# Sums of an MLP's second layer: kept in SBUF and added by VectorE, or kept in DRAM and added by accumulating DMAs

## The chip, the cores and the metric

The kernel runs on one core of a Trainium2 chip, in one launch. Its time is the device time of an execution in microseconds (us). The number compared is a median over runs.

## The reference

Three layers follow one another, on 2 x 768 = 1536 tokens of 512 features, all in float32:

```python
x = attention(q, k, v)                  # window of 16 keys each side, and block summaries
h = x @ w_in                            # 512 -> 2048, "first layer"
g = np.maximum(h, 0.0) + np.log1p(np.exp(-np.abs(h)))
x2 = g @ w_out                          # 2048 -> 512, "second layer"
a = x2 @ w1                             # 512 -> 1024
b = x2 @ w2
out = (a * b @ w3) @ w_out2             # 1024 -> 1024 -> 512
```

The change touches how `x2` is summed.

## The kernel before

Matrix products run with float32 values split into a high and a low part, three matmuls in place of one (`mm3`, line 239). w3 and the last matrix are multiplied with each other once, "w34", so that the last layer is one product. The tokens are worked on in 3 chunks c of 512.

The second layer sums over 16 blocks of 128 features of g. PSUM (2 banks for the first layer, 4 for the second, 2 others) has no room for sums of all three chunks at once, so the blocks go in 4 groups of four. A stage s = 0 to 11 is one group (s // 3) of one chunk (s % 3). Within it, steps X{n}, n = 4s to 4s+3, add up in four banks, one for each output block o of 128 features. At the end of a stage the banks must be emptied before the next one can begin. X{4s+3} is the last step into the banks, X{4s+4} the first of the next stage.

Before, the step Xo{s}_{o} empties a bank into one of 12 rows r = 4c + o. These lie in four SBUF tiles `acc` of three rows each, which are held until the end of the second layer. In the first group, it is a copy (`X_first`: VectorE for even o, line 545, ScalarE for odd o, line 543). In the later groups VectorE adds the bank to its row (`X_out`, line 549). After that a row is split into high (`x2_hi`, line 554, ScalarE) and low parts (`x2_lo`, line 557, GpSimd). For chunks 1 and 2 the last layers use a scheme of seven products P1 to P7 in place of eight, for which VectorE forms sums of rows in place (`T_sum`, line 646), and their low parts (line 672).

The seven products are done for i = 0 to 7 (`prod`, line 710); P1_1 is product 1 of i = 1. Each has a PSUM bank, of four in turn. VectorE combines them (`plus`, line 726: U2, U3, U4, C11, C12, C22, C21), and whichever operation reads a bank last frees it. It also does what the next i needs: sums of the weight tiles (Sf, line 680, and Ss, line 687, with low parts Sl, line 694), the gating product Mb (line 730), the low part Pl of the gated values (line 739) and half of the output copies Oo (line 744).

All steps are sorted once, on the host, by a planner (`Order`) with a cost per step, a latency per engine and the number of buffers of each kind. It emits the steps in its order of start times, and every engine executes its own part of that in order. The steps of TensorE have given places. Temporary tiles of 128 x 512 come from one pool `tmp` of 4 buffers: the softplus values `tm` between the two layers, `pa`, `t1`, `u` and `osb` later. A step that takes a buffer waits until the last user of the one that had it before is done.

Of the kernel before, what the change touches and what calls it, by code (L numbers as in the profile page):

```python
# [8 lines left out]
F32 = mybir.dt.float32  # L9
# [5 lines left out]
ALU = mybir.AluOpType  # L15
# [8 lines left out]
class Order:  # L24
# [21 lines left out]
    def add(self, name, eng, cost, place, fn, needs=(), take=(), give=(), port=False, table=None, lead=0.0):  # L46
        assert name not in self.steps, name
        self.steps[name] = (eng, cost, place, fn, list(dict.fromkeys(d for d in needs if d)), list(take))
        self.extra[name] = (port or eng == "POOL", table, lead)
        for t, b in take:  # L50
            assert b not in self.owner, b
            self.owner[b] = t
        for b in give:
            self.users.setdefault(b, {})[name] = 1
# [150 lines left out]
def fused_kernel(ctx, tc, q, k, kwin, v, vb, w_in, w_out, w1, w2, w3, wo2, mask, sel, ident, out):  # L205
    nc = tc.nc
    P = 128
    B, NT, _, NP, _, _ = q.shape
# [5 lines left out]
    CH = 512  # L214
# [6 lines left out]
    tmp_p = ctx.enter_context(tc.tile_pool(name="tmp", bufs=4))  # L221
# [3 lines left out]
    acc_p = ctx.enter_context(tc.tile_pool(name="acc", bufs=4))  # L225
# [3 lines left out]
    dr = ctx.enter_context(tc.tile_pool(name="dr", bufs=1, space=bass.MemoryType.DRAM))  # L229

    w34_d = dr.tile([8, P, D], F32, name="w34_d")
    vs_d = [dr.tile([NBK, D], F32, name=f"vs_d{b}") for b in range(B)]

    def f(ap):
# [66 lines left out]
    xt = {}  # L301
# [187 lines left out]
    xps = {}  # L489
    acc = {}  # L490
    x2 = {}

    def step(n):

        return n // 12, n % 12 // 4, 4 * (n // 12) + n % 4
# [37 lines left out]


    def acc_row(r):
        if r // 3 not in acc:
            acc[r // 3] = acc_p.tile([P, 3, CH], F32, tag="acc", name="acc")
        return acc[r // 3][:, r % 3]

    def X_first(s, o):  # L540
        a, p = acc_row(4 * s + o), xps[s, o]
        if o % 2:
            nc.scalar.copy(a, p)
        else:
            nc.vector.tensor_copy(a, p)

    def X_out(s, o):
        a = acc_row(4 * (s % 3) + o)
        nc.vector.tensor_tensor(a, a, xps[s, o], ALU.add)

    def x2_hi(c, o):
        if c not in x2:
            x2[c] = xt_p.tile([P, 2, 4, CH], F32R, tag="xt", name="x2t")
        nc.scalar.copy(x2[c][:, 0, o], acc_row(4 * c + o))

    def x2_lo(c, o, eng):
        eng.tensor_tensor(x2[c][:, 1, o], acc_row(4 * c + o), f(x2[c][:, 0, o]), ALU.subtract)
# [87 lines left out]
    def T_sum(t, k):  # L645
        sub = lambda d, a, b: nc.vector.tensor_tensor(d, a, b, ALU.subtract)
        if t == 1:
            tf[1, k] = tmp_p.tile([P, CH], F32, tag="tmp", name="t1")
            sub(tf[1, k], acc_row(8 + k), acc_row(4 + k))
        elif t == 3:  # L650
            sub(acc_row(8 + k), acc_row(10 + k), acc_row(8 + k))
        elif t == 2:
            sub(acc_row(10 + k), acc_row(10 + k), tf[1, k])
        else:
            sub(acc_row(6 + k), acc_row(6 + k), acc_row(10 + k))

    def T_hi(t, k):
        if (t, 0) not in tt:
            if t == 1:
                tt[1, 0] = acc_p.tile([P, 2, CH], F32R, tag="acc", name="t1h")  # L660
                tt[1, 1] = st_p.tile([P, 2, CH], F32R, tag="st", name="t1l")
            elif t == 3:
                tt[3, 0], tt[3, 1] = rows(2, 0, 0), rows(2, 1, 0)
            else:
                y = xt_p.tile([P, 2, 4, CH], F32R, tag="xt", name="t24")
                for a in range(2):
                    tt[2, a], tt[4, a] = y[:, a, 0:2], y[:, a, 2:4]
        nc.scalar.copy(tt[t, 0][:, k], tf[1, k] if t == 1 else acc_row({3: 8, 2: 10, 4: 6}[t] + k))

    def T_lo(t, k):  # L670
        src = tf[1, k] if t == 1 else acc_row({3: 8, 2: 10, 4: 6}[t] + k)
        nc.vector.tensor_tensor(tt[t, 1][:, k], src, f(tt[t, 0][:, k]), ALU.subtract)
# [75 lines left out]
    def O_store(c, m):  # L748
# [5 lines left out]
    o = Order({"h": 2, "x": 4, "a": 2, "xt": 3, "wi": 6, "wo": 6, "g": 4, "tmp": 4, "st": 4, "cv": 3, "acc": 4,  # L754
               "kw": 3, "q": 3, "s": 3, "b": 8, "c": 2})
    add = o.add
# [150 lines left out]
    for j in jobs:  # L907
        kind, i, p = j
# [60 lines left out]
    for n in range(N1):  # L969
        g, c, i = step(n)  # L970
# [13 lines left out]
    for s_ in range(12):  # L984
        g, c = divmod(s_, 3)
        for o_ in range(4):
            r = 4 * c + o_
            if g == 0:
                add(f"Xo{s_}_{o_}", "ACT" if o_ % 2 else "DVE", .6, None, lambda s_=s_, o_=o_: X_first(s_, o_),
                    (f"X{4*s_+3}_{o_//2}", f"Xo{(r-r%3)//4}_{(r-r%3)%4}" if r % 3 else None),  # L990
                    () if r % 3 else [("acc", f"acc{r//3}")], (f"x{s_}_{o_}",))
            else:
                add(f"Xo{s_}_{o_}", "DVE", .68, None, lambda s_=s_, o_=o_: X_out(s_, o_),
                    (f"X{4*s_+3}_{o_//2}", f"Xo{s_-3}_{o_}"), (), (f"x{s_}_{o_}",))
            if g == 3 and (c < 2 or o_ > 1):
                add(f"x2h{c}_{o_}", "ACT", .62, None, lambda c=c, o_=o_: x2_hi(c, o_),
                    (f"Xo{s_}_{o_}", o_ % 2 and f"x2h{c}_{o_-1}", c < 2 and o_ and f"x2h{c}_0"), () if o_ != 2 * (c == 2) else [("xt", f"y{c}")])
                add(f"x2l{c}_{o_}", "POOL", 1.3, None, lambda c=c, o_=o_: x2_lo(c, o_, nc.gpsimd),
                    (f"x2h{c}_{o_}",), (), (f"acc{r//3}",), lead=2)


    for r in range(16):
        p, jp = divmod(r, 4)
# [3 lines left out]
    for i in range(8):  # L1007
        p = i // 2
# [3 lines left out]
        p = ("acc", "st", "wi", "wi", "wi", "wi", "c", "c")[i]  # L1012
# [15 lines left out]

    A = lambda *rs: sorted({f"acc{r//3}" for r in rs})
    for k_ in range(2):  # L1030
        add(f"T1s{k_}", "DVE", .68, None, lambda k_=k_: T_sum(1, k_), (f"Xo11_{k_}", f"Xo10_{k_}"),
            [("tmp", f"tx{k_}")], A(8 + k_, 4 + k_), port=True)
        add(f"T3s{k_}", "DVE", .68, None, lambda k_=k_: T_sum(3, k_), (f"T1s{k_}", f"Xo11_{2+k_}"), (), A(8, 9, 10, 11), port=True)
        add(f"T2s{k_}", "DVE", .68, None, lambda k_=k_: T_sum(2, k_), (f"T3s{k_}", f"x2l2_{2+k_}"), (), A(10, 11), port=True)
        add(f"T4s{k_}", "DVE", .68, None, lambda k_=k_: T_sum(4, k_), (f"T2s{k_}", f"x2l1_{2+k_}"), (), A(6, 7, 10, 11), port=True)
        for t, src, tk in ((1, [f"tx{k_}"], [("acc", "t1h"), ("st", "t1l")]), (3, A(8 + k_), []), (2, A(10 + k_), [("xt", "y3")]), (4, A(6 + k_), [])):
            first_ = k_ == 0 and t in (1, 2)
            add(f"T{t}h{k_}", "ACT", .62, None, lambda t=t, k_=k_: T_hi(t, k_),
                (f"T{t}s{k_}", "x2h2_2", k_ and f"T{t}h0", t == 1 and f"T2s{k_}", t == 4 and "T2h0"), tk if first_ else (), lead=8 if t in (1, 3) else 0)
            add(f"T{t}l{k_}", "DVE", .68, None, lambda t=t, k_=k_: T_lo(t, k_), (f"T{t}h{k_}",), (), src, port=True)  # L1040
# [49 lines left out]
    for n in range(N2):  # L1090
        c, i = divmod(n, 8)
# [84 lines left out]
```

## Time and profile before

| | |
|---|---|
| median of 3 runs | 565.78 us (564.92 to 566.63) |
| span of the profiled execution | 564.7 us; its own time beside it is not recorded |
| TensorE busy | 544.2 us (96%) |
| VectorE busy | 403.3 us (71%) |
| ScalarE busy | 319.3 us (57%) |
| GpSimd busy | 157.8 us (28%) |
| DMA, mean over the span | 108 GB/s |

The span is measured from the first to the last instruction of the profiled execution. The difference between it and the median of the runs is 1.1 us. Busy shares are means over the whole kernel, whose stages differ: attention until some 84 us, the two layers of the first MLP to 376 us (with the weights' conversion beside it), the gated product of chunk 0 to 437 us, the seven-product scheme to some 533 us, and the last output. In the windows view each engine's busy time is given by stage.

### The profile page before, as it was taken

How to read it: one execution, taken by the hardware profiler on the slowest of the kernel's cores; microseconds unless marked ns; L12 is line 12 of the kernel's file. 1: busy time of each engine (PE TensorE's matmuls, PEld its weight loads, DVE VectorE, ACT ScalarE, POOL GpSimd, SP SyncE). 2: the span in 40 equal slices, each digit the busy share in tenths (PEclk: the TensorE clock that was granted, in tenths of full speed). 3: DMA queues.
4: the chain of work that ended last, by engine and by line, in shares of the span. 5: the costliest groups of instructions: out<-in, count | busy, mean ns of one | idle time of the engine just before them, and what ended most of it. 6: DMA issues, size and time to landing. Idle time of an engine off the chain costs nothing.

```text
span 564.7 us, 8599 instructions
## 1 busy us (share of the span) xinstructions
PE 544.2 (96%) x3154; PEld 446.3 (79%) x3154; DVE 403.3 (71%) x789; ACT 319.3 (57%) x685; POOL 157.8 (28%) x144
## 2 busy tenths in 40 slices
PE   8768799999999999999999999999999999999997
PEld 4657588888888888888888888888888888888885
DVE  4787899668777677765776655676687799989710
ACT  4788877667777666665655656566653233222310
POOL 2565634113343242303230243146462000000000
PEclk9898999999999999999999999999999999999999
DMA  9898934224454443414242512235300010000021
GB/s 319 289 251 196 244 113 150 82 68 157 142 149 118 144 140 122 150 39 148 89 135 74 150 49 84 93 104 170 112 25 1 19 56 2 0 1 0 2 93 57
DMA packets 22804, 61.22 MB, mean 108 GB/s; under 512 B 3145, under 2 KB 3593, under 8 KB 22761
## 3 DMA queue, kind: packets, MB, share of 16 engines
q1 hardware_dynamic: 22760, 60.66, 35.3%
q8 instruction: 25, 0.41, 0.3%
q14 instruction: 19, 0.15, 0.1%
HBM read 55.31 MB, written 5.34 MB: 107 GB/s over the span
## 4 chain that ended last, share of the span: by engine, by line
PE 92%; ACT 5%; DVE 2%; issue 1%; POOL 0%; POOLq 0%
PE hps L239 23%; PE xps L239 23%; PE abps L710 14%; PE ops L239 12%; PE abps L239 8%; PE wps L239 8%; ACT s L425 4%; PE av L466 2%; PE z_p L854 1%; PE tr L445 1%; PE sc L407 1%; DVE at L454 1%; ACT at L452 0%; DVE s L419 0%; DVE ks L313 0%
## 5 line engine op out<-in xcount | busy, mean ns | idle before, releaser
L286 POOL TENSOR_TENSOR w<-cv,w 128x512 fp32r<-128x512 f32 x72 | 98.1, 1365 | 222.8 <-ACT w L282 212.1
L239 PE MATMUL hps<-xt,w 128*128 128x512 f32 x576 | 138.5, 390 | 0.0
L239 PE MATMUL xps<-gt,w 128*128 128x512 f32 x576 | 137.7, 389 | 0.0
L239 PEld LDWEIGHTS xps<-gt,w 128*128 128x128 f32 x576 | 108.1, 188 | 22.4
L239 PEld LDWEIGHTS hps<-xt,w 128*128 128x128 f32 x576 | 107.8, 188 | 22.6 <-POOL w L286 0.3
L511 DVE SCALAR_TENSOR_TENSOR tm<-tm,hps 128x512 f32<-128x512 f32 x48 | 32.9, 687 | 53.2 <-ACT tm L508 53.1
L239 PE MATMUL ops<-w,pt 128*128 128x512 f32 x288 | 67.6, 389 | 0.0
L278 DVE SCALAR_TENSOR_TENSOR cv<-cv,raw 128x512 int32<-128x512 int32 x72 | 59.9, 833 | 9.9 <-ACT cv L272 8.1
L239 PEld LDWEIGHTS ops<-w,pt 128*128 128x128 f32 x288 | 54.1, 188 | 11.2
L508 ACT ACTIVATE tm<-hps 128x512 f32<-128x512 f32 x48 | 28.6, 598 | 58.2 <-PE hps L239 58.1
L266 DVE SCALAR_TENSOR_TENSOR raw<-raw 128x512 int32<-128x512 int32 x72 | 57.8, 803 | 4.9 <-ACT raw L262 4.8
L282 ACT CAST w<-cv 128x512 fp32r<-128x512 f32 x72 | 44.4, 619 | 16.7 <-DVE cv L278 11.8
L262 ACT ACTIVATE raw<-raw 128x512 int32<-128x512 uint16 x69 | 46.2, 670 | 2.3 <-DMA raw<-in_w_in_dram 1.5
L239 PE MATMUL wps<-w 128*128 128x512 f32 x192 | 46.1, 389 | 0.0
L239 PE MATMUL abps<-x2t,w 128*128 128x512 f32 x192 | 44.5, 389 | 0.0
L272 ACT ACTIVATE cv<-raw 128x512 f32<-128x512 f32 x64 | 42.3, 662 | 0.0
L239 PEld LDWEIGHTS wps<-w 128*128 128x128 f32 x192 | 36.0, 188 | 7.5
L239 PEld LDWEIGHTS abps<-x2t,w 128*128 128x128 f32 x192 | 36.0, 188 | 7.5
L517 DVE SCALAR_TENSOR_TENSOR hps<-hps,tm 128x512 f32<-128x512 f32 x48 | 33.3, 696 | 10.2 <-ACT tm L514 8.6
L425 ACT ACTIVATE s<-s,sm 128x120 f32<-128x120 f32 x96 | 36.7, 387 | 6.5 <-DVE sm L419 6.5
L524 DVE TENSOR_TENSOR gt<-hps,gt 128x512 fp32r<-128x512 f32 x48 | 33.1, 689 | 7.6 <-ACT gt L521 6.4
L521 ACT CAST gt<-hps 128x512 fp32r<-128x512 f32 x48 | 28.2, 588 | 14.6 <-DVE hps L517 14.5
(85 smaller groups left out, 664.1 us busy)
## 6 DMA issues: line engine op xcount, KB each, us to landing
raw<-in_w_dram SPq DMA_DIRECT2D x32, 512.0 KB, 3.5
raw<-in_w_in_dram SPq DMA_DIRECT2D x16, 512.0 KB, 4.2
raw<-in_w_out_dram SPq DMA_DIRECT2D x16, 512.0 KB, 10.3
vw<-in_v_dram SPq DMA_DIRECT2D x12, 384.0 KB, 10.7
raw<-in_wo_dram SPq DMA_DIRECT2D x8, 512.0 KB, 3.6
kt<-in_k_dram SPq DMA_DIRECT2D x4, 768.0 KB
qt<-in_q_dram SPq DMA_DIRECT2D x12, 256.0 KB, 5.6
vt<-in_v_dram SPq DMA_DIRECT2D x4, 768.0 KB, 7.7
```

Of the source, the lines that this page charges most:

```text
L239: nc.tensor.matmul(ps, lhs(a), rhs(b), start=first and i == 0, stop=last and i == 2)
L262: nc.scalar.activation(r[:, :, 0], r.bitcast(U16)[:, :, 1], AF.Copy, bias=-(0.5 - 2.0 ** -14), scale=2.0 ** -13)
L266: nc.vector.scalar_tensor_tensor(r[:, :, 0], r[:, :, 1], -0x80000000, r[:, :, 0], ALU.bitwise_and, ALU.bitwise_or)
L272: nc.scalar.activation(f(c), h, AF.Copy, scale=2.0 ** -112)
L278: nc.vector.scalar_tensor_tensor(c, c, 3, r[:, :, 0], ALU.logical_shift_left, ALU.bitwise_or)
L282: nc.scalar.copy(w[:, 0], f(cvs[kind, i]))
L286: eng.tensor_tensor(w[:, 1], f(cvs[kind, i]), f(w[:, 0]), ALU.subtract)
L425: nc.scalar.activation(s[:, e], s[:, e], AF.Exp, bias=sm[:, 0, e:e + 1], scale=-1.0, accum_out=sm[:, 1, e:e + 1])
L511: nc.vector.scalar_tensor_tensor(tm[n], tm[n], -2.0, hps[n], ALU.mult, ALU.add)
L517: nc.vector.scalar_tensor_tensor(hps[n], hps[n], 0.0, tm[n], ALU.max, ALU.add)
L524: nc.vector.tensor_tensor(gt[n][:, 1], hps[n], f(gt[n][:, 0]), ALU.subtract)
L710: nc.tensor.matmul(ps, w[:, a, (o + kk) * P:(o + kk + 1) * P], rhs(b), start=kk == 0 and n == 0, stop=kk == 1 and n == 2)
```

## The change

Twelve tiles `x2_d` in DRAM take the place of the held SBUF rows while sums are formed. Xo{s}_{o} is now always a copy of the bank (`X_copy`, VectorE for even o, ScalarE for odd) into a tile `xo` of the pool `tmp`. A new step Xs{s}_{o} (`X_sum`) moves it to DRAM: in the first group a plain store from SyncE's queue (12 of them), in the later three groups a DMA from GpSimd's queue that adds to what is there (36). After the last, a step Xl{r} loads each row into an `acc` tile (12 loads from SyncE's queue). The high parts and the sums T1s and T3s now need the load. The planner is given 1.1 and 0.7 us for the new steps; the rest of its table is as before.

```diff
+    x2_d = [dr.tile([P, CH], F32, name=f"x2_d{r}") for r in range(12)]
...
-    def X_first(s, o):
-        a, p = acc_row(4 * s + o), xps[s, o]
-        if o % 2:
-            nc.scalar.copy(a, p)
-        else:
-            nc.vector.tensor_copy(a, p)
-
-    def X_out(s, o):
-        a = acc_row(4 * (s % 3) + o)
-        nc.vector.tensor_tensor(a, a, xps[s, o], ALU.add)
+    def X_copy(s, o):
+        xo[s, o] = tmp_p.tile([P, CH], F32, tag="tmp", name="xo")
+        if o % 2:
+            nc.scalar.copy(xo[s, o], xps[s, o])
+        else:
+            nc.vector.tensor_copy(xo[s, o], xps[s, o])
+
+    def X_sum(s, o):
+        r = 4 * (s % 3) + o
+        if s < 3:
+            nc.sync.dma_start(x2_d[r], xo[s, o])
+        else:
+            nc.gpsimd.dma_start(x2_d[r], xo[s, o], accum_op=ALU.add)
+
+    def X_load(r):
+        if r % 3 == 0:
             acc[r // 3] = acc_p.tile([P, 3, CH], F32, tag="acc", name="acc")
+        nc.sync.dma_start(acc_row(r), x2_d[r])
...
+            add(f"Xo{s_}_{o_}", "ACT" if o_ % 2 else "DVE", .6, None, lambda s_=s_, o_=o_: X_copy(s_, o_),
+                (f"X{4*s_+3}_{o_//2}",), [("tmp", f"xo{s_}_{o_}")], (f"x{s_}_{o_}",))
+            add(f"Xs{s_}_{o_}", "POOL" if g else "SP", 1.1 if g else .7, None, lambda s_=s_, o_=o_: X_sum(s_, o_),
+                (f"Xo{s_}_{o_}", g and f"Xs{s_-3}_{o_}"), (), (f"xo{s_}_{o_}",), lead=2 if g == 3 else 0)
+            if g == 3:
+                add(f"Xl{r}", "SP", .7, None, lambda r=r: X_load(r), (f"Xs{s_}_{o_}", r % 3 and f"Xl{r-r%3}"),
+                    () if r % 3 else [("acc", f"acc{r//3}")], lead=2)
...
-        add(f"T1s{k_}", "DVE", .68, None, lambda k_=k_: T_sum(1, k_), (f"Xo11_{k_}", f"Xo10_{k_}"),
+        add(f"T1s{k_}", "DVE", .68, None, lambda k_=k_: T_sum(1, k_), (f"Xl{8+k_}", f"Xl{4+k_}"),
```

The order of TensorE's instructions stays as it was. VectorE's moves in places where nothing was edited. The first place is in the seven-product scheme at i = 0. In VectorE's order before, U2_0 (the first row) is followed by the weight sums Sf1 and Ss1 of i = 1 and by C11_0, which reads bank abps_4330; then come U3_0, U4_0, C22_0 and C12_0:

```order
L726 TENSOR_TENSOR u_4326<-u_4317,abps_4310 128x512
L680 TENSOR_TENSOR fs_4328<-w_3564 128x512
L680 TENSOR_TENSOR fs_4339<-w_3582 128x512
L687 TENSOR_TENSOR fs_4339<-fs_4339 128x256
L687 TENSOR_TENSOR fs_4339<-fs_4328,fs_4339 128x256
L687 TENSOR_TENSOR fs_4328<-fs_4339,fs_4328 128x256
L726 TENSOR_TENSOR u_4317<-u_4317,abps_4330 128x512
L726 TENSOR_TENSOR u_4359<-u_4326,abps_4343 128x512
L726 TENSOR_TENSOR u_4326<-u_4326,u_4337 128x512
L726 TENSOR_TENSOR u_4337<-u_4337,u_4359 128x512
L726 TENSOR_TENSOR u_4326<-u_4326,abps_4352 128x512
L730 TENSOR_TENSOR u_4326<-u_4326,u_4337 128x512
```

The same place in the changed kernel, from U3_0 on (lines are 9 higher; C11_0 is the row that reads abps_4442, the row of L753 is the output copy Oo01, that of L748 is Pl16, and the last is C21_0):

```order
L735 TENSOR_TENSOR u_4471<-u_4449,abps_4455 128x512
L735 TENSOR_TENSOR u_4449<-u_4449,u_4453 128x512
L735 TENSOR_TENSOR u_4453<-u_4453,u_4471 128x512
L735 TENSOR_TENSOR u_4449<-u_4449,abps_4464 128x512
...
L739 TENSOR_TENSOR u_4449<-u_4449,u_4453 128x512
...
L696 TENSOR_TENSOR fs_4486<-fs_4493,fs_4486 128x256
L735 TENSOR_TENSOR u_4428<-u_4428,abps_4442 128x512
L753 COPY osb_4509<-ops_4037 128x512
L696 TENSOR_TENSOR fs_4486<-fs_4486 128x256
L748 TENSOR_TENSOR pt_4504<-u_4449,pt_4504 128x512
L735 TENSOR_TENSOR u_4471<-u_4471,abps_4474 128x512
```

The weight sums of i = 1 (the two Sf stand in the first gap, two of the three Ss in the second) and C11_0 have moved from ahead of U3_0 to behind C12_0 and Mb16, and an output copy and Pl16 stand ahead of C21_0. What took their place ahead of U3_0 are sums and low parts of the T rows and of the weights of i = 0, which come later than before (not shown).

The second place is the same engine at the end of i = 1, before and then after. Before, from C12_1 to Sl20 (the first and the last row):

```order
L726 TENSOR_TENSOR u_4441<-u_4441,abps_4457 128x512
L730 TENSOR_TENSOR u_4441<-u_4441,u_4451 128x512
L687 TENSOR_TENSOR fs_4455<-fs_4455 128x256
L687 TENSOR_TENSOR fs_4455<-fs_4453,fs_4455 128x256
L687 TENSOR_TENSOR fs_4453<-fs_4455,fs_4453 128x256
L687 TENSOR_TENSOR fs_4453<-fs_4453 128x256
L739 TENSOR_TENSOR pt_4486<-u_4441,pt_4486 128x512
L726 TENSOR_TENSOR u_4464<-u_4464,abps_4467 128x512
L694 TENSOR_TENSOR s2_4507<-fs_4453,s2_4507 128x512
```

After, with fs_4598 the weight sum Sf21:

```order
L735 TENSOR_TENSOR u_4561<-u_4561,abps_4575 128x512
L689 TENSOR_TENSOR fs_4598<-w_3852 128x512
L739 TENSOR_TENSOR u_4561<-u_4561,u_4571 128x512
L696 TENSOR_TENSOR fs_4598<-fs_4598 128x256
L696 TENSOR_TENSOR fs_4598<-fs_4573,fs_4598 128x256
L696 TENSOR_TENSOR fs_4573<-fs_4598,fs_4573 128x256
L696 TENSOR_TENSOR fs_4573<-fs_4573 128x256
L748 TENSOR_TENSOR pt_4610<-u_4561,pt_4610 128x512
L735 TENSOR_TENSOR u_4582<-u_4582,abps_4585 128x512
L703 TENSOR_TENSOR s2_4627<-fs_4573,s2_4627 128x512
```

Sf21 has come in between C12_1 (the first row) and Mb17; before, it stood ahead of U3_1.

The third place is VectorE at the end of the first stage that adds (stage 3), here of the changed kernel with what each instruction waits for:

```order
L546 COPY xo_2147<-xps_1941 128x512 [waits PE_49]
L512 SCALAR_TENSOR_TENSOR tm_2128<-tm_2128,hps_2087 128x512 [waits DMAHW6_49,Activation_49]
L546 COPY xo_2159<-xps_1958 128x512 [waits DMASW0_49,PE_49,Activation_49]
L518 SCALAR_TENSOR_TENSOR hps_2087<-hps_2087,tm_2128 128x512 [waits Activation_49]
L267 SCALAR_TENSOR_TENSOR raw_2051<-raw_2051 128x512 [waits DMAHW2_49,Activation_49]
L525 TENSOR_TENSOR gt_2172<-hps_2087,gt_2172 128x512 [waits Activation_49]
L512 SCALAR_TENSOR_TENSOR tm_2187<-tm_2187,hps_2134 128x512 [waits DMASW1_49,DVE_49,Activation_49]
```

There four adds (line 549) stood before. Now Xo3_0 and Xo3_2 are copies, and Xo3_2 and a later softplus step each wait for a DMA of GpSimd's queue (DMASW), whose tile they take over.

## Rows read from the trace of the kernel before

**Rows 1.** Page: busy us (share of the span) xinstructions.
```profile
PE 544.2 (96%) x3154; PEld 446.3 (79%) x3154; DVE 403.3 (71%) x789; ACT 319.3 (57%) x685; POOL 157.8 (28%) x144
```

**Rows 2.** Windows by stage: length, then each engine's busy us.
```profile
80.00:376.00 296.00, 296.00 (x1308) 245.11 (x1307) 208.63 (x308) 195.01 (x340) 88.81 (x66) 1.00 0.37 114
...
437.00:465.00 28.00, 28.00 (x125) 22.97 (x124) 23.84 (x41) 8.42 (x15) 0.00 (x0) 1.00 0.10 38
465.00:500.00 35.00, 35.00 (x156) 28.99 (x155) 32.10 (x56) 10.05 (x17) 0.00 (x0) 1.00 0.01 1
```

**Rows 3.** Waits of TensorE's weight loads from 80 us on: all there is.
```profile
PEld abps L710 <- DVE s L694: 0.3, 1, 0.3
```

**Rows 4.** Lines by form, 80 to 376 us: busy, mean ns, idle before.
```profile
L286 POOL TENSOR_TENSOR w<-cv,w 128x512 fp32r<-128x512 f32 x61 | 82.8, 1361 | 199.8 <-ACT w L282 189.0 <-issue 10.7
...
L549 DVE TENSOR_TENSOR acc<-acc,xps 128x512 f32<-128x512 f32 x35 | 22.1, 681 | 2.4 <-PE xps L239 2.4
...
L545 DVE COPY acc<-xps 128x512 f32<-128x512 f32 x6 | 4.1, 686 | 0.6 <-PE xps L239 0.6
L543 ACT COPY acc<-xps 128x512 f32<-128x512 f32 x6 | 3.5, 588 | 2.2 <-PE xps L239 2.2
```

**Rows 5.** Timeline, seven-product scheme, end of i = 0: start, length, instructions.
```profile
441.87 1.29 DVE L680 TENSOR_TENSOR fs<-w 128x512 f32<-128x512 f32 x2
...
443.19 1.34 DVE L687 TENSOR_TENSOR fs<-fs 128x256 f32<-128x256 f32 x3
...
443.71 2.88 PE L710 MATMUL abps<-x2t,s 128*128 128x512 f32 x12
444.45 1.51 DVE L726 TENSOR_TENSOR u<-u,abps 128x512 f32<-128x512 f32 x2
446.07 1.42 DVE L726 TENSOR_TENSOR u<-u 128x512 f32<-128x512 f32 x2
...
447.40 0.68 DVE L726 TENSOR_TENSOR u<-u,abps 128x512 f32<-128x512 f32 x1
...
450.29 2.68 PEld L710 LDWEIGHTS abps<-x2t,w 128*128 128x128 f32 x12
450.51 2.88 PE L710 MATMUL abps<-x2t,w 128*128 128x512 f32 x12
```

**Rows 6.** Timeline at the end of i = 1, around the one wait.
```profile
463.88 1.29 DVE L694 TENSOR_TENSOR s<-fs,s 128x512 fp32r<-128x512 f32 x2
...
464.62 0.77 PEld L710 LDWEIGHTS abps<-t,s 128*128 128x128 f32 x4 [0.32 <-DVE s L694]
```

**Rows 7.** Timeline around the end of stage 3: X15, then X16.
```profile
166.28 2.88 PE L239 MATMUL xps<-gt,w 128*128 128x512 f32 x12
...
171.72 2.88 PE L239 MATMUL xps<-gt,w 128*128 128x512 f32 x12
```

**Rows 8.** DMA issues: KB each, median us from issue to landing.
```profile
raw<-in_w_out_dram SPq DMA_DIRECT2D x16, 512.0 KB, 10.3
...
out_dram<-osb SPq DMA_DIRECT2D x12, 256.0 KB, 2.0
...
w34r<-w_d SPq DMA_DIRECT2D x8, 256.0 KB, 3.3
```

**Rows 9.** Waits of GpSimd: us in total, times, longest.
```profile
POOL w L286 <- issue: 10.7, 3, 4.2
```

**Rows 10.** Tiles acc and x2t: duration min/median/max ns, first and last start us.
```profile
L554 ACT CAST x2t<-acc x10: 612/620/623, 328.9 to 415.0; 128x512 fp32r<-128x512 f32 x10
L557 POOL TENSOR_TENSOR x2t<-acc,x2t x10: 1295/1382/1739, 329.6 to 423.7; 128x512 fp32r<-128x512 f32 x10
...
L646 DVE TENSOR_TENSOR t<-acc x2: 686/1229/1772, 404.5 to 413.4; 128x512 f32<-128x512 f32 x2
...
L239 PE MATMUL abps<-x2t,w x192: 389/389/389, 375.7 to 432.6; 128*128 128x512 f32 x192
```

More of the change, by code (lines that the diff above doesn't have):

```diff
@@ L535, in acc_row @@
     def acc_row(r):
-        if r // 3 not in acc:
-            acc[r // 3] = acc_p.tile([P, 3, CH], F32, tag="acc", name="acc")
-        return acc[r // 3][:, r % 3]
-    def X_first(s, o):
-        a, p = acc_row(4 * s + o), xps[s, o]
-        if o % 2:
-            nc.scalar.copy(a, p)
-        else:
-            nc.vector.tensor_copy(a, p)
-    def X_out(s, o):
-        a = acc_row(4 * (s % 3) + o)
-        nc.vector.tensor_tensor(a, a, xps[s, o], ALU.add)
+        return acc[r // 3][:, r % 3]
+    xo = {}
+    def X_copy(s, o):
[12 more added lines that the diff above has]
+        if r % 3 == 0:
+            acc[r // 3] = acc_p.tile([P, 3, CH], F32, tag="acc", name="acc")
+        nc.sync.dma_start(acc_row(r), x2_d[r])
     def x2_hi(c, o):
@@ L987, in fused_kernel @@
             r = 4 * c + o_
[L988 to L994, printed above, removed]
+            add(f"Xo{s_}_{o_}", "ACT" if o_ % 2 else "DVE", .6, None, lambda s_=s_, o_=o_: X_copy(s_, o_),
[5 more added lines that the diff above has]
+                    () if r % 3 else [("acc", f"acc{r//3}")], lead=2)
             if g == 3 and (c < 2 or o_ > 1):
                 add(f"x2h{c}_{o_}", "ACT", .62, None, lambda c=c, o_=o_: x2_hi(c, o_),
-                    (f"Xo{s_}_{o_}", o_ % 2 and f"x2h{c}_{o_-1}", c < 2 and o_ and f"x2h{c}_0"), () if o_ != 2 * (c == 2) else [("xt", f"y{c}")])
+                    (f"Xl{r}", o_ % 2 and f"x2h{c}_{o_-1}", c < 2 and o_ and f"x2h{c}_0"), () if o_ != 2 * (c == 2) else [("xt", f"y{c}")])
                 add(f"x2l{c}_{o_}", "POOL", 1.3, None, lambda c=c, o_=o_: x2_lo(c, o_, nc.gpsimd),
@@ L1030, in fused_kernel @@
     for k_ in range(2):
-        add(f"T1s{k_}", "DVE", .68, None, lambda k_=k_: T_sum(1, k_), (f"Xo11_{k_}", f"Xo10_{k_}"),
+        add(f"T1s{k_}", "DVE", .68, None, lambda k_=k_: T_sum(1, k_), (f"Xl{8+k_}", f"Xl{4+k_}"),
             [("tmp", f"tx{k_}")], A(8 + k_, 4 + k_), port=True)
-        add(f"T3s{k_}", "DVE", .68, None, lambda k_=k_: T_sum(3, k_), (f"T1s{k_}", f"Xo11_{2+k_}"), (), A(8, 9, 10, 11), port=True)
+        add(f"T3s{k_}", "DVE", .68, None, lambda k_=k_: T_sum(3, k_), (f"T1s{k_}", f"Xl{10+k_}"), (), A(8, 9, 10, 11), port=True)
         add(f"T2s{k_}", "DVE", .68, None, lambda k_=k_: T_sum(2, k_), (f"T3s{k_}", f"x2l2_{2+k_}"), (), A(10, 11), port=True)
```

## Prediction

> **What bounds the kernel now.** I read the page's busy times first: TensorE 544.2 of 564.7 us, every other engine far below [rows 1]. Those are means, so next the windows by stage. TensorE is busy for all of 80 to 376 us, where the change is made, and also of 437 to 465 and 465 to 500 us [rows 2]. Its weight loads wait once after 80 us, for 0.3 us [rows 3]. So no VectorE time that the change saves can shorten the kernel by more than these 0.3 us; the question is whether it makes TensorE wait. The same windows say where that is near: VectorE is busy for 71% of the long stage, but for 85% of 437 to 465 us and for 92% of the 35 us behind it [rows 2]. There a delay of VectorE is not made up soon, and it frees the banks that TensorE writes.
>
> **Removed and added work.** 36 adds of 681 ns leave VectorE, 24 us, and 18 copies of 686 ns come, 12 us; ScalarE gets 18 copies of 588 ns, 11 us [rows 4]. Over 296 us with VectorE busy for 209 and ScalarE for 195, under a TensorE that has no gap [rows 2], both cost and gain nothing. 12 stores and 12 loads on SyncE's queue only carry data; their cover is below. GpSimd gets 36 issues of DMAs that add. No row shows one. The nearest of GpSimd's rows is its own operation of 1.36 us [rows 4], and 36 of these are 49 us on an engine busy for 89 of 296 [rows 2], which for most of its idle time waits for ScalarE, 189 us [rows 4]. Behind an issue that waits for its copy stand the low parts of converted weights; their delay is that of one copy, under 1 us, and TensorE did not wait for a weight once [rows 3]. I cost that at nothing; if that cover were thin, each late conversion would cost up to 1 us.
>
> **The way from the last sum to its user.** It becomes copy, adding DMA, load, high part. For chunk 0 the high parts began at 328.9 us and the products that need them at 375.7 [rows 10], 47 us of cover for two DMAs, of 3.3 us for a load after a store [rows 8] or 10.3 for the slowest row [rows 8]. For chunk 2 the last banks are read by 376 us, and the first T sum was at 404.5 [rows 10], 28 us. Nothing on TensorE, then; but the T sums and the low parts come later in VectorE's order, and that is where the price arises.
>
> **P1_1 waits for C11_0.** VectorE's order at the end of i = 0 is new. P1_1 writes into the bank that C11_0 reads. Before, C11_0 was at 444.45 and the matmuls of P1_1 at 450.51, with 5 us to spare [rows 5]. Now C11_0 stands behind nine others that come after U3_0. U3_0 can't come sooner: it reads P7_0, the first six of the twelve matmuls from 443.71, and so keeps its start, the second of the pair, 444.45 + 1.51 - 0.69 = 445.27 [rows 5]. The work ahead of it does not hold it up: from U2_0, which reads P6_0's bank and starts at 441.87 - 0.6 = 441.27, it is two T low parts and one Pl at 0.6 each, done by 443.7. From there, by the same rows: U4_0 446.07, C22_0 446.80, C12_0 447.40; then Sf10 and Sf11 at steps of 0.60 (the pair of 1.29 less one of 0.69), 448.00 and 448.60; Mb16 449.20; Ss11 449.80, Ss31 and Ss21 at steps of 0.46 (1.34 for three of 0.42), 450.26 and 450.72; C11_0 0.34 after the last (443.19 + 0.92 to 444.45), 451.06 to 451.74 [rows 5]. The row of the one wait shows 0.05 us from the end of VectorE's operation (463.88 + 0.69) to the weight load at 464.62 [rows 6], and the matmul follows its load by 0.22 [rows 5]: 452.0 in place of 450.5, **1.5 us**.
>
> **P2_1 waits for C21_0.** Its bank is freed by C21_0, which now has Oo01, Ss41 and Pl16 between C11_0 and itself: 451.06 + 0.60 + 0.60 + 0.34 + 0.60 = 453.20, end 453.88, matmul at 454.15. P1_1 would be done issuing at 452.0 + 6 x 0.226 = 453.36, as twelve take 2.88 us [rows 5]: **0.8 us**. The low parts Sl10 and Sl11 that P6_1 and P5_1 need then end some 0.8 and 0.3 us ahead of these, by the same steps.
>
> **P6_2 waits for Sl20**, as it did for 0.3 us [rows 3, 6]. Between C12_1 and Sl20 stands one more operation, Sf21; C12_1 follows a bank of TensorE as before, and the rows from there on are without a pause. One step of 0.60: **0.6 us**. From i = 2 on, the two orders are the same, and all later work moves together.
>
> **X16 waits for a DMA.** This is the term that no row gives. Xo3_2, which empties a bank for X16, takes the tile of Xo3_1, and so waits until the first adding DMA has landed. Xo3_1 may begin when the first six matmuls of X15 are done, 166.28 + 5 x 0.226 + 0.39 = 167.80 [rows 7, 10]; with 0.59 for the copy [rows 4] and two times 0.05 the issue is at 168.5. The bank goes to X16's fourth output block, its tenth matmul, 171.72 + 9 x 0.226 = 173.75 [rows 7]. Xo3_2's 0.69, the 0.05 and the load's 0.22 lie before it, so the wait is issue to landing less 4.3 us. Ends: a landing 2.0 after issue, as for a store [rows 8], none; 10.3, the slowest row of a DMA [rows 8], 6.0; and as issue alone was seen to take 4.2 us on GpSimd [rows 9], 4.2 + 3.3 - 4.3 = 3.2. The nearest rows are GpSimd's operation for the issue, 1.36 [rows 4], and a load that follows a store for the transfer, 3.3 [rows 8]: 4.7, and I take **0.4 us**. Later stages take tiles from DMAs too, with 3 to 5 us more before TensorE would notice (estimate from the same spacing of 5.4 us between X steps [rows 7]).
>
> **Sum.** 1.5 + 0.8 + 0.6 + 0.4 = 3.3 us on a span of 564.7. The median lies 1.1 above that span, and I let it: 564.7 + 1.1 + 3.3 = **569.1 us**.
>
> **A rule against it.** GpSimd's low parts of x2 took 1.30 us at least and 1.74 at most [rows 10], so what runs beside it can hold GpSimd up by 0.4 us. The Trainium skill, SBUF — State Buffer, "A bandwidth-pool intuition that's wrong (but worth ruling out)", goes further: a DMA issued from GpSimd needs its descriptors written by GpSimd, which VectorE's two-port operations lock out, so that 620 ns became 3100 beside a copy. By this page's figures, as an estimate, 2.5 us more per issue. No row here shows a DMA from GpSimd, so the trace does not decide it. The copies of the change read PSUM, and take 686 ns, no less than an add of two operands [rows 4], which does not look like the fast form that the rule speaks of.
>
> **Rivals.**
> (a) The adding DMAs land late, from 7 us after issue on, because GpSimd is held while it issues. For it: an issue wait of 4.2 us [rows 9]. Against: 0.4 us is what its operations were stretched by [rows 10]. X16 then waits 2.7 us at 7 us and 6.0 at 10.3, in place of 0.4: 571.4 to 574.7, more if a second stage is late. Chance 0.2.
> (b) Not slower: VectorE reaches C11_0 and C21_0 in time, because P1_1 and P2_1 get banks that were freed sooner than I read, or the weight sums are not in the way. It decides from a C11_0 that ends by 450.2; my chain ends 1.5 us later, of which the five weight sums are 2.5. Then 0.6 to 1.0 are left: 566.4 to 566.8, within 0.3%. For it: before, these banks had 5 us to spare [rows 5]. Against: the order, and U3_0's tie to TensorE. Chance 0.2.
> (c) The change doesn't keep SyncE's or GpSimd's queue clear: a weight's load or low part is late in the long stage, and TensorE stops there several times for 1 us. For it: weights land after 10.3 us [rows 8]. Against: the idle time of GpSimd [rows 4]. Some 571 to 575. Chance 0.07.
> The forecast has 0.53.
>
> **How the numbers follow.** 0.3% of 565.78, about what a measurement of this kernel tells from no change, is 1.7 us: 564.1 to 567.5. (b) lies within it, and as TensorE has no gap to close but 0.3 us I give only 0.03 of its 0.2 to faster; with 0.02 of the forecast, where the waits come out at half their size, no change has 0.19. The rest of the forecast, (a) and (c) are slower, 0.78. The range reaches down into (b) and up to X16's wait at 8 to 9 us of landing: 566.3 to 573.3. The forecast's own is 567.7 to 570.7: P1_1 and P2_1 together 1 us less or more, X16 from nothing to 1.
>
> **What would show it.** Right: TensorE's weight loads wait at line 719 (the products) near 451 us for line 735 on VectorE (1.4 to 1.5 and 0.8), near 467 for line 703 (0.9), and at 173 to 174 us for line 546 (under 1); VectorE's busy time falls by 12 us without use. Wrong: no wait at the products, which is (b); waits for line 546 or 544 of several us, or DMAs of GpSimd's queue with over 7 us to landing, which is (a); waits for line 287, which is (c).

## The result and the profile after

The changed kernel takes 569.77 us (median of 5 runs, 568.64 to 570.67) against 565.78: a ratio of 1.0064 with a 95% interval of 1.0049 to 1.0080, so 2.8 to 4.5 us slower. The forecast was 569.1 us, with a range of 566.3 to 573.3.

The page's busy times after, as in [rows 1], and the windows of the stages in [rows 2]:

```profile
PE 546.4 (96%) x3154; PEld 447.0 (79%) x3154; DVE 398.6 (70%) x771; ACT 327.4 (58%) x703; POOL 193.2 (34%) x180
```

```profile
80.00:376.00 296.00, 295.82 (x1306) 244.58 (x1305) 199.32 (x288) 199.57 (x350) 116.04 (x96) 1.00 0.59 155
...
437.00:470.00 33.00, 31.06 (x135) 24.74 (x134) 30.39 (x53) 10.02 (x18) 0.00 (x0) 1.00 0.09 33
```

VectorE gave back 9 us in the long stage, where nobody waited for it (over the whole kernel only 4.7: from 376 to 437 us its operations took longer, 49 of them 44.8 us, where before 56 took 44.7). TensorE, which had no gap, now has 0.2 us of gaps there and 1.9 in the stage of the seven products. All waits of the weight loads from 80 us on, which were one row before [rows 3]:

```profile
PEld abps L719 <- DVE u L735: 2.5, 2, 1.5
PEld abps L719 <- DVE s L703: 0.8, 1, 0.8
PEld xps L240 <- DVE xo L546: 0.6, 1, 0.6
```

These are the four places of the forecast and no other. The timeline there, as in [rows 5, 6] (VectorE's C11_0, the load for P1_1, C21_0, the load for P2_1; then Sl20 with Sl21, and the load for P6_2):

```profile
451.06 0.68 DVE L735 TENSOR_TENSOR u<-u,abps 128x512 f32<-128x512 f32 x1
...
451.79 1.23 PEld L719 LDWEIGHTS abps<-x2t,w 128*128 128x128 f32 x6 [1.54 <-DVE u L735]
...
453.19 0.68 DVE L735 TENSOR_TENSOR u<-u,abps 128x512 f32<-128x512 f32 x1
...
453.92 1.22 PEld L719 LDWEIGHTS abps<-x2t,w 128*128 128x128 f32 x6 [0.91 <-DVE u L735]
...
466.52 1.29 DVE L703 TENSOR_TENSOR s<-fs,s 128x512 fp32r<-128x512 f32 x2
...
467.26 0.76 PEld L719 LDWEIGHTS abps<-t,s 128*128 128x128 f32 x4 [0.78 <-DVE s L703]
```

C11_0 starts at 451.06 and C21_0 at 453.19, where the steps put them (451.06 and 453.20). That the times agree to the hundredth is in part luck: the attention stage ran 0.50 us shorter in this trace, which the 0.46 lost at X16 nearly cancels. What the steps worked out is the way from U3_0 (445.27 in both) to C11_0, 5.79 us, and this came as they said. And X16 [rows 7], with GpSimd's first adding DMA, Xo3_2, and the rest of X16:

```profile
168.26 1.01 POOL L553 DMA_DIRECT2D x_d<-xo  x1 [2.57 <-PE xps L240]
...
172.87 0.69 DVE L546 COPY xo<-xps 128x512 f32<-128x512 f32 x1 [4.62 <-DMA x_d<-xo]
...
173.61 0.53 PEld L240 LDWEIGHTS xps<-gt,w 128*128 128x128 f32 x3 [0.60 <-DVE xo L546]
```

From issue to the copy that waits it takes 172.87 - 168.26 = 4.6 us.

A wait of the loads is longer than what TensorE loses, since loads run ahead. So I compare starts: the same matmul, counted from the first of the 3154, in a trace and in that of before, and how the difference grows. In this trace it is -0.50 at 75 us (the attention stage ran that much shorter; over the traces below this start differs by 1.7 us, so the spans of two traces say less than these steps), and then:

| trace | at 75 us | X16 | P1_1 | P2_1 | P6_1 to P6_2 |
|---|---|---|---|---|---|
| after | -0.50 | +0.46 | +1.28 | +0.89 | +0.46 |
| order of before | +0.09 | +0.49 | 0 | 0 | 0, but +4.6 at P6_0 and P5_0 |
| order alone | -1.30 | 0 | +1.28 | +0.91 | +0.47 |
| own tiles | -1.53 | 0 | +1.51 | +0.89 | +0.47 |
| plain DMAs | -1.54 | 0 | +1.28 | +0.89 | +0.47 |
| last add on VectorE | -0.67 | +0.46 | 0 | 0 | 0 |
| weight loads first | -0.29 | +0.40 | +1.29 | +0.90 | +0.49 |
| first landing later | -1.22 | +3.02, then +1.74 | +1.28 | +0.89 | +0.47 |
| two moved up | +0.11 | +0.49 | 0 | 0 | +1.98 |

After: 0.46 + 1.28 + 0.89 + 0.46 = 3.1 us. The spans differ by 3.0, as the -0.50 ahead and 0.4 behind the last matmul nearly cancel. The rest of the table is read below.

### The profile page after: what moved, and what is told of

Read it like the earlier page. It is cut to its first block, busy times and chain, and to the rows that moved or that the text cites. A ratio compares the mean times of both kernels' runs of the same rounds, so it can differ in the third digit from the quotient of the medians.

```text
span 567.8 us, 8835 instructions
## 1 busy us (share of the span) xinstructions
PE 546.4 (96%) x3154; PEld 447.0 (79%) x3154; DVE 398.6 (70%) x771; ACT 327.4 (58%) x703; POOL 193.2 (34%) x180
## 3 DMA queue, kind: packets, MB, share of 16 engines
q0 software_dynamic: 5184, 9.44, 11.5%
## 4 chain that ended last, share of the span: by engine, by line
PE 81%; DVE 7%; ACT 5%; DMA 4%; issue 2%; POOL 1%; DVEq 0%; SPq 0%; POOLq 0%
PE xps L240 21%; PE hps L240 20%; PE abps L719 12%; PE ops L240 11%; PE abps L240 8%; PE wps L240 7%; DMA raw<-in_w_in_dram 3%; ACT s L426 3%; PE z_p L863 1%; DVE u L735 1%; DVE raw L267 1%; DMA x_d<-xo 1%; PE tr L446 1%; DVE cv L279 1%; PE av L467 1%
## 5 line engine op out<-in xcount | busy, mean ns | idle before, releaser
L287 POOL TENSOR_TENSOR w<-cv,w 128x512 fp32r<-128x512 f32 x72 | 101.3, 1408 | 160.1 <-ACT w L283 155.3
L267 DVE SCALAR_TENSOR_TENSOR raw<-raw 128x512 int32<-128x512 int32 x72 | 60.4, 839 | 14.7 <-ACT raw L263 14.6
L553 POOL DMA_DIRECT2D x_d<-xo x36 | 32.8, 1052 | 38.0 <-DVE xo L546 32.7
```

What stands on the lines that cost most here:

```text
L267: nc.vector.scalar_tensor_tensor(r[:, :, 0], r[:, :, 1], -0x80000000, r[:, :, 0], ALU.bitwise_and, ALU.bitwise_or)
L287: eng.tensor_tensor(w[:, 1], f(cvs[kind, i]), f(w[:, 0]), ALU.subtract)
```

## The experiments

Ratios are to the kernel before as it ran beside the experiments: a median of 566.62 us for the first three, 566.72 for "last add on VectorE". The other four ran once, for their traces.

**The order of before, put back.** The steps from about 391 us on are emitted in a list; a table of names stands for the planner's order.

```diff
-    names = o.order()
+    names = ORDER        # changed kernel up to its last row load, then as before
```

> The changed kernel, with the order of the steps from about 391 us on (gated products, T sums, seven products, outputs) as it was before the change; copies, adding DMAs and loads stay. Theory (the loss is VectorE's new order in the seven-product scheme): the waits of TensorE for C11_0 (1.5 us by the profile) and C21_0 (0.9) are gone, that for Sl20 is 0.3 again, X16's wait for the adding DMA stays at 0.4 to 0.6; the time falls by 2.4 to 2.7 us against the changed kernel, to 567.0 to 567.5 (ratio to before 1.001 to 1.003). Rival (the DMAs themselves cost it, by their queue or their traffic): no more than 0.5 us comes back, 569.3 to 569.8 (1.006 to 1.007).

Measured: ratio 1.0107 (1.0087 to 1.0127), 572.49 us: slower still, which neither theory had. Its waits of the weight loads:

```profile
PEld abps L799 <- issue: 2.2, 1, 2.2
PEld abps L799 <- DVE t L761: 1.0, 1, 1.0
PEld xps L320 <- DVE xo L626: 0.7, 1, 0.7
PEld abps L799 <- DVE s L783: 0.3, 1, 0.3
```

C11_0 and C21_0 are waited for no more, as I said, but P6_0, at 442 to 443 us, now waits for VectorE twice: for the last gating product of chunk 0 (line 703), which frees its bank, and for a low part of the T rows (line 761). The waits of the matmuls themselves say so:

```profile
PE abps L799 <- DVE pa L703: 1.8, 1, 1.8
PE abps L799 <- DVE t L761: 0.6, 1, 0.6
```

By the starts of matmuls this costs 4.6 us, 2.9 at the two waits and some 1.7 behind them, where the clock fell (see the last section). VectorE is late there with its T sums too, by the tile `acc` (first and last start; 406.3 to 436.1 us before):

```profile
L735 DVE TENSOR_TENSOR acc<-acc x4: 684/690/693, 417.5 to 444.4; 128x512 f32<-128x512 f32 x4
```

With the change in place the old order comes too late, and the planner's new one is the cheaper of the two, 2.6 us at the products against 4.6. So "VectorE's new order" is how the loss comes about, not where it begins.

**The new order without the DMAs.**

```diff
-    names = o.order()
+    names = ORDER        # of the changed kernel, without Xs and Xl; kernel before otherwise
```

> The kernel before, adds on VectorE into rows in SBUF and no DMA for them, with all steps in the order of the changed kernel (its stores, adding DMAs and loads left out of the list). Theory: TensorE waits at the same three places as in the changed kernel, 1.5, 0.9 and 0.8 us, and nowhere at X16; 2.4 to 2.7 us over before, 568.2 to 568.5 (ratio 1.004 to 1.005). Rival (the DMAs): as before, 565.8 (0.999 to 1.001), no such waits.

Measured: ratio 1.0044 (1.0029 to 1.0059), 569.08 us, 2.5 more. The waits:

```profile
PEld abps L788 <- DVE u L804: 2.5, 2, 1.5
PEld abps L788 <- DVE s L772: 0.8, 1, 0.8
```

The same two rows as in the changed kernel, to a tenth, with every sum in SBUF and no DMA for it. The rival fell: what is lost at the products is not the DMAs' traffic.

**Tiles of their own for the copies of stages 3 to 8.**

```diff
-        xo[s, o] = tmp_p.tile([P, CH], F32, tag="tmp", name="xo")
+        xo[s, o] = (acc_p if 3 <= s < 9 else tmp_p).tile([P, CH], F32, tag="acc" if 3 <= s < 9 else "tmp", name="xo")
```

> The changed kernel, with the copies of stages 3 to 8 in tiles of the pool acc, which is idle then, in place of tiles of tmp; same order. Theory: X16's wait for the adding DMA (0.6 us by the profile) is gone, since Xo3_2 has a tile of its own; the three waits at the products stay at 1.5, 0.9 and 0.8; 0.4 to 0.5 us less than the changed kernel, 569.2 to 569.5. Rival (the tiles held by DMAs are what costs most): 2 to 4 us less, 566 to 568.

Measured: ratio 1.0063 (1.0037 to 1.0088), 569.62 us, too wide to tell 0.5 us. The trace does: the wait at X16 is gone, the others are there.

```profile
PEld abps L719 <- DVE u L735: 2.7, 2, 1.8
PEld abps L719 <- DVE s L703: 0.8, 1, 0.8
```

P1_1 waits 0.2 us longer here. U3_0, at the head of the way to C11_0, shows why, in the changed kernel and then here:

```profile
445.27 0.69 DVE L735 TENSOR_TENSOR u<-u,abps 128x512 f32<-128x512 f32 x1 [1.24 <-PE abps L719]
```

```profile
443.96 0.69 DVE L735 TENSOR_TENSOR u<-u,abps 128x512 f32<-128x512 f32 x1
```

In the changed kernel VectorE waits for P7_0 and starts 1.56 us behind its first matmul (443.71). Here it comes without a pause and 1.80 behind it (442.16): its own work ahead of U3_0 was not done in time.

**Plain DMAs on GpSimd's queue.** The addition is left out.

```diff
-            nc.gpsimd.dma_start(x2_d[r], xo[s, o], accum_op=ALU.add)
+            nc.gpsimd.dma_start(x2_d[r], xo[s, o])
```

> The changed kernel with plain DMAs in place of adding ones on GpSimd's queue; the addition is left out, so rows hold the last group alone. If the landing of 5.4 us (median) comes from the addition, which must read what is there: 2 to 3.3 us to landing as for the plain stores and loads, and X16 does not wait. If it comes from the issue by GpSimd: 4.5 to 5.5 us to landing, and X16 waits 0.3 to 0.6 us. Either way the three waits at the products stay at 1.5, 0.9 and 0.8.

Measured: 2.6 us to landing (median), and X16 does not wait; the time of the one execution was 568.15 us. The rows of the DMAs after, and of this kernel (KB each, median us to landing), and the time of an issue on GpSimd (min/median/max ns) in the same two:

```profile
x_d<-xo POOLq DMA_DIRECT2D x36, 256.0 KB, 5.4
...
L553 POOL DMA_DIRECT2D x_d<-xo x36: 858/948/1567, 168.3 to 385.3; - x36
```

```profile
x_d<-xo POOLq DMA_DIRECT2D x36, 256.0 KB, 2.6
...
L553 POOL DMA_DIRECT2D x_d<-xo x36: 539/539/710, 167.2 to 382.1; - x36
```

So the addition costs 2.8 us of landing and 0.4 of issue; that GpSimd issues it costs little, 2.6 us against 2.0 for a store of the same size from SyncE's queue [rows 8].

**The last add on VectorE.** Rows are loaded before the last group, and VectorE adds its banks to them (stages 9 to 11), as before the change.

```diff
+            if g < 3:
+                ...
+            else:
+                add(f"Xl{r}", "SP", .7, None, lambda r=r: X_load(r), (f"Xs{s_-3}_{o_}", r % 3 and f"Xl{r-r%3}"),
+                    () if r % 3 else [("acc", f"acc{r//3}")], lead=8)
+                add(f"Xo{s_}_{o_}", "DVE", .68, None, lambda s_=s_, o_=o_: X_out(s_, o_),
+                    (f"X{4*s_+3}_{o_//2}", f"Xl{r}"), (), (f"x{s_}_{o_}",))
```

> Rows of chunk sums stay in DRAM for the first three groups (12 stores, 24 adding DMAs); they are loaded before the last group, whose banks VectorE adds to them, as before the change. The planner then gives VectorE the order of the kernel before from 391 us on. Theory (rows of the last chunk come late because of the way copy, DMA, load, and so VectorE's work slides into its full stretch): TensorE waits at X16 for 0.5 us and for Sl20 for 0.3, and at neither C11_0 nor C21_0; 0.2 to 0.8 us over before, ratio 1.000 to 1.0015, 2.5 to 3 us under the changed kernel. Rival (adding DMAs cost by themselves): two thirds of the changed kernel's loss remain, ratio 1.004.

Measured: ratio 1.0003 (0.9986 to 1.0019), 567.46 us, no difference to before that this measurement can tell, with 24 of the 36 adding DMAs still there. Its waits and its first T sums:

```profile
PEld xps L240 <- DVE xo L546: 0.6, 1, 0.6
PEld abps L723 <- DVE s L707: 0.3, 1, 0.3
```

```profile
L659 DVE TENSOR_TENSOR t<-acc x2: 689/1230/1770, 404.3 to 413.3; 128x512 f32<-128x512 f32 x2
```

The T sums are where they were before [rows 10], and the three waits with them. This is the step that settles where the loss begins: not that sums lie in DRAM, but what the last group's way there and back brings with it. It takes away copies, adding DMAs and late row loads together, and so does not say which of them.

**Weight loads ahead of the row loads in SyncE's queue.** In the changed kernel SyncE waited 23.6 us for adding DMAs from 360 to 420 us, and two weight loads behind it went out at 391.38 and 393.91. SyncE's issues before, there, and ScalarE and VectorE, which have the weight next:

```profile
379.09 1.81 SPq L248 DMA_DIRECT2D raw<-in_w_dram  x2
```

```profile
390.96 0.32 SPq L558 DMA_DIRECT2D acc<-x_d  x1
391.38 0.38 SPq L249 DMA_DIRECT2D raw<-in_w_dram  x1
393.49 0.32 SPq L558 DMA_DIRECT2D acc<-x_d  x1
393.91 0.38 SPq L249 DMA_DIRECT2D raw<-in_w_dram  x1
395.79 0.66 ACT L263 ACTIVATE raw<-raw 128x512 int32<-128x512 uint16 x1 [5.64 <-DMA raw<-in_w_dram]
396.48 0.69 DVE L267 SCALAR_TENSOR_TENSOR raw<-raw 128x512 int32<-128x512 int32 x1 [5.82 <-ACT raw L263]
```

```diff
-    names = o.order()
+    names = ORDER        # wl2, lw15, lw25 moved ahead of Xl9, all else the same
```

> The changed kernel, with the next two weight loads and the w34 load ahead of the last six row loads in SyncE's queue; all other engines keep the changed kernel's order. In the changed kernel SyncE waited for adding DMAs there, and ScalarE 5.6 us for a weight (at 395.8). If that queue is what makes the rows late: ScalarE's wait falls to under 1 us, the first T sum (412.1 us) moves to 406 to 408, and as VectorE's order is the same, TensorE still loses 1.3, 0.9 and 0.5 us at the three products. If the DMAs' way alone makes them late: the first T sum stays at 410 to 412. If lateness in itself and not the order costs: less than 1 us is lost at the products.

Measured (one execution, 569.90 us), ScalarE's wait and the first T sum; then the T sums of the changed kernel and of "order alone":

```profile
393.01 0.67 ACT L343 ACTIVATE raw<-raw 128x512 int32<-128x512 uint16 x1 [2.73 <-DMA raw<-in_w_dram]
```

```profile
L735 DVE TENSOR_TENSOR t<-acc x2: 1195/1488/1781, 410.2 to 418.9; 128x512 f32<-128x512 f32 x2
```

```profile
L655 DVE TENSOR_TENSOR t<-acc x2: 1191/1484/1778, 412.1 to 420.8; 128x512 f32<-128x512 f32 x2
```

```profile
L724 DVE TENSOR_TENSOR t<-acc x2: 685/785/885, 407.9 to 416.7; 128x512 f32<-128x512 f32 x2
```

Between my cases, and by the T sum at the edge of the second: the wait is halved and the T sum comes 1.9 us sooner (412.1 to 410.2), of the 7.6 by which it was late. The traces together say more. The weight load that SyncE issues at 379.09 before, and the first T sum:

| trace | weight load issued | first T sum |
|---|---|---|
| last add on VectorE | 378.90 | 404.3 |
| before | 379.09 | 404.5 |
| order alone | 383.63 | 407.9 |
| weight loads first | 387.46 | 410.2 |
| after | 391.38 | 412.1 |
| order of before | 392.52 | 415.7 |

The T sums are late as this load is late. They do not wait for the rows: the last row load of the changed kernel goes out at 393.49 and the row loads land after 2.6 us (median), 16 us ahead of the first T sum. VectorE stood still for 5.8 us until 396.48 for the weight, and had its conversions to make up before the T sums. The order alone, with no row in DRAM, already makes 3.4 of the 7.6 us. In "weight loads first" the load is still 8 us late, behind a w34 load (385.51 for 377.74 before) and for a buffer that VectorE has to free; why these are late was not tested. The losses at the products did not move, as these rest on VectorE's order once that is set.

**The first landing later.**

```diff
+            for _ in range(4 * ((s, o) == (3, 1))):
+                nc.gpsimd.tensor_tensor(scr, xo[s, o][:, :256], xo[s, o][:, 256:], ALU.add)
             nc.gpsimd.dma_start(x2_d[r], xo[s, o], accum_op=ALU.add)
```

> The changed kernel, with four operations of 128 x 256 on GpSimd (some 0.7 us each) between the copy Xo3_1 and its adding DMA, the first of the kernel, and nowhere else. By my step for X16 (wait = issue to landing, counted from the copy, less a fixed cover), TensorE loses 0.46 + 2.7 = 3.2 us at X16 in place of 0.46, and nothing more elsewhere: the three products as before, 1.3, 0.9, 0.5. If other work ends the wait at X16 (VectorE's own queue), it grows by less than 1 us.

Measured:

```profile
167.28 3.19 POOL L555 TENSOR_TENSOR scr<-xo 128x256 f32<-128x256 f32 x4 [2.33 <-ACT xo L545]
...
170.41 1.01 POOL L556 DMA_DIRECT2D x_d<-xo  x1
...
175.55 1.45 PE L240 MATMUL xps<-gt,w 128*128 128x512 f32 x3 [2.86 <-DVE xo L547]
...
176.80 4.05 PE L240 MATMUL wps<-w 128*128 128x512 f32 x12
```

The time of the one execution was 573.17 us. Its VectorE has Xo3_2 at

```profile
174.80 0.69 DVE L547 COPY xo<-xps 128x512 f32<-128x512 f32 x1 [7.31 <-DMA x_d<-xo]
```

Counted from the start at 75 us (this trace is 0.72 us ahead of that of the changed kernel), the issue came 2.87 us later, 170.41 for 168.26, and Xo3_2 2.65 later, 174.80 for 172.87. The matmul that waits for it lost 3.02 us, in the changed kernel 0.34: 2.68 more. So the wait does follow the landing one for one. What I had not counted are 1.74 us behind it (0.12 in the changed kernel); see the last section.

**C11_0 and C21_0 moved up.**

```diff
-    names = o.order()
+    names = ORDER        # C11_0 ahead of U3_0, C21_0 behind C12_0
```

> The changed kernel with two operations of VectorE moved up: C11_0 ahead of U3_0, C21_0 right behind C12_0; all else in the same order. Theory by steps: no wait for C11_0 and C21_0; but the weight sums behind them are later by these two, so that the next reader waits: Sl10, at 453.7 to 454.4 by the durations of the rows, for P6_1 at 453.2, 1.2 to 1.5 us, and 0.5 at Sl20; 1.7 to 2.0 us lost in place of 2.6. Rival (the two banks are all there is): 0.5 us lost.

Measured (one execution, 569.61 us): no wait for the banks, but three for low parts of the weights and one for their high part, and 1.98 us lost between P6_1 and P6_2 in place of 2.64. The sum is as I said, its parts are not: P6_1 lost 0.9, and P5_1, which I had not named, 0.6.

```profile
PEld abps L799 <- DVE s L783: 2.0, 3, 0.8
PEld abps L799 <- ACT s L780: 0.7, 1, 0.7
```

VectorE is late there as a whole: what was moved up handed three quarters of the loss to what stood behind it.

## Why the prediction was right

The time lay 0.7 us from the forecast, and every wait came where a step had put it. The sizes came less well than the sum: P1_1 and P6_2 were put too high, P2_1 and X16 too low, and the four together at 3.3 us for 3.1.

- No gain: TensorE had no gap for VectorE's 12 us. Shown, by the windows. The 12 us themselves came as 9 in the long stage and 4.7 in all.
- P1_1 for C11_0: 1.5 forecast, 1.28 lost. C11_0 came to the hundredth; the load began 0.05 us after it, but the first matmul is recorded with its load at 451.79 and not 0.22 behind it. That was the term's error.
- P2_1 for C21_0: 0.8 forecast, 0.89 lost.
- P6_2 for Sl20: 0.6 forecast, 0.46 lost.
- X16 for the adding DMA: 0.4 forecast, from 4.7 us of issue to landing; 0.46, and 4.6. It was worked out from 1.36 for the issue and 3.3 for the landing behind it. The sum was right for this DMA, the first, whose issue took 1.01 us. It is in part luck, as both parts were taken from rows of other work: the median adding DMA took 5.4 us, and by the same step X16 would have waited 1.1 for one of these.
- What lies around the span: I let it stay at 1.1 us. The profiled execution after took 569.61 us for a span of 567.8, 1.8 around it. So some 0.7 us of the difference between forecast and median come from here. By that the execution whose trace I had of before took 566.5 us, which is what later runs of that kernel took (566.62 and 566.72): the first median, 565.78, was a little low.

Of the rivals, (a) did not come: the median landing is 5.4 us and the longest 9.8. Five of the 36 took over 7 us, one of the signs that I had named for (a), but of TensorE's steps X16 alone waited for one. ScalarE waited for tiles held by adding DMAs, and TensorE did not notice it:

```profile
ACT tm L509 <- DMA x_d<-xo: 8.2, 4, 2.5
```

Two of the readings for (a) were wrong. The 4.2 us of [rows 9] are not the issue of a DMA: GpSimd issued none before, and the view calls idle time "issue" for which it shows no other engine. And 10.3 us is not the slowest row of a DMA; the page has one of 10.7. The lock-out of GpSimd by VectorE, from the Trainium skill (SBUF — State Buffer, "A bandwidth-pool intuition that's wrong (but worth ruling out)"), is not seen in these runs: beside the same work of VectorE, plain DMAs from GpSimd's queue kept it for 0.54 to 0.71 us each and landed after 2.6 us (median). (b) failed as VectorE's order bound it. (c) came in part, with another effect: SyncE's queue was blocked, and no weight was late for TensorE, but one was for ScalarE and VectorE, and the T sums behind it.

One step was right in its result and thin in its reason. I took the loads on SyncE's queue as only carrying data, and asked whether the last rows come in time: 28 us of cover. That cover held, for TensorE and for the T sums. What I did not ask is what stands behind a row load in its queue. Two weight loads did, and went out 12 to 13 us later than before, and VectorE's T sums came 7.6 us later (412.1 for 404.5) and slid from a stretch with room into one with none. "Order alone" and "last add on VectorE" show the two ends of this: the order makes the loss at the products without DMAs, and with the last group added on VectorE the planner keeps the old order (VectorE's 194 operations from 391 us on are those of before, one for one) and that loss is gone, with 24 adding DMAs. Which of the new steps made the planner choose the other order was not tested.

## What to carry to other kernels

Where one engine never waits, work taken off another gains nothing; look instead for what the change makes late. Follow a late value past the engine that bounds the kernel, to the engine that prepares its operands: if that engine has its full stretch just behind, the slack of the first is no cover. Ask of each DMA that has to wait not only who needs it, but what stands behind it in its queue. And here a sum kept in DRAM cost little while its last addend was added on the chip; what cost was the round trip between the last addend and the first use, with all that it put off.

## What the runs showed of the hardware

An adding DMA of 256 KB from GpSimd's queue landed 5.4 us (median) after its issue, a plain one 2.6 after, and its issue kept GpSimd for 0.95 us in place of 0.54. The same 9.44 MB were moved in more packets, which took more of the DMA engines' time (packets, MB, share of 16 engines; with the addition, then without):

```profile
q0 software_dynamic: 5184, 9.44, 11.5%
```

```profile
q0 software_dynamic: 2880, 9.44, 4.4%
```

A wait of 2.9 us cost TensorE more than 2.9 us. Where X16's wait was made longer, the granted clock fell behind it; the windows of that kernel at 172 to 180 and 180 to 190 us:

```profile
172.00:180.00 8.00, 5.14 (x17) 3.74 (x16) 4.66 (x8) 3.68 (x7) 3.35 (x4) 0.79 0.86 111
180.00:190.00 10.00, 10.00 (x46) 8.28 (x45) 6.83 (x11) 6.91 (x13) 4.45 (x3) 1.00 0.66 182
```

The column after POOL is the clock, 0.79 on the mean, so a part of the stretch ran at the lower level, 1.2 GHz. Twelve matmuls there took 4.05 us, where 2.88 is their time at full clock, and the last of X16 ahead of them were slow too: 1.6 us on top of the wait (1.74 less the 0.12 of the changed kernel). In "order of before" the clock fell behind two waits of TensorE close to each other, of 1.8 and 0.6 us:

```profile
444.00:446.00 2.00, 2.00 (x6) 1.52 (x5) 2.00 (x4) 0.87 (x2) 0.00 (x0) 0.50 0.04 8
```

In the changed kernel the clock stayed at 1.00 in the windows of 172 to 180 and of 437 to 470 us, beside the waits of 0.6 to 1.5 us.
